# A change of order on two engines: FFN maximum against bias bands on VectorE, left-over keys against AV on TensorE

## The chip, the cores and the metric

The kernel runs on one core of one Trainium2 chip. The metric is device time in microseconds (us) of one execution. Five engines of the core matter here: TensorE (PE in the profile; PEld are its weight loads), VectorE (DVE), ScalarE (ACT), GpSimd (POOL, which here issues the casting loads) and SyncE (SP, which issues stores and DMA transposes). Lines such as L350 are lines of the kernel's source.

## The reference, cut to what matters

Attention with a relative-position bias per head over 8 batches x 8 heads x 576 tokens x 64, then a maxout FFN with three products over the 4608 tokens.

```python
scores = q @ k.T / sqrt(D) + bias[bucket(|i - j|)]        # per batch and head
attn = exp(scores - max) / sum(exp(scores - max))
x = (attn @ v).transpose(...).reshape(B * S, H * D)
h = maximum(maximum(x @ w1, x @ w2), x @ w3)              # [4608, 768]
out = h @ w_out                                           # [4608, 512]
```

## The kernel before

Heads go in pairs: a *step* (b, hp) is batch b and head pair hp, both counted from 0. A step has two halves. Each half is a *visit* (scores of four key tiles against 256 queries on TensorE, exponentials on ScalarE), bias *bands* (VectorE multiplies tile t of the exponentials by exp(bias); only tiles near the diagonal need it), one half of the AV product of the step before, and one *portion* of the FFN of the batch before. 576 is 4 x 128 + 64: the last 64 keys and queries of a head are handled apart, as *left-overs*.

```python
ps_f = ctx.enter_context(tc.tile_pool(name="ps_f", bufs=2, space=PSUM))    # FFN banks
...
def first(fb):       # f: product with w1; ScalarE copies it to m0
    ...
def second(fb):      # m: product with w2; VectorE: m = max(ps1, m0)
    ...
def third(fb):       # g: product with w3; VectorE: hT = max(ps2, m)
    ...
# portions of 512 tokens: [rest, f0, m0], [g0, f1, m1], ... [g4, f5, m5], [g5, None, o0], [o1, o2]

def fill(target, *hooks):      # FFN groups of the next portions, hooks in between
    ...
    for j, group in enumerate(groups):
        while hooks and (j == len(groups) - 1 or j > 0 and len(hooks) > len(groups) - 1 - j):
            hooks.pop(0)()
        group()
    for hook in hooks:
        hook()

def transposes(b):             # SyncE: DMA transposes of a batch's q and k, one t per call
    ...
    for t in range(KT + 1):    # t == KT: the left-over tiles
        one(0, t)              # qT
        one(1, t)              # kT
        yield

def left_keys(hp, qT, kT, el, lo, hi, sc=None):
    ...
        mm(sc[:, q0 - lo : q1 - lo], lhsT=kT[:, KT * P :], rhs=qT[:, q0:q1])
    exp(el[:, lo:hi], sc[:, 0 : hi - lo])
...
    # one step
    together = b > 1 and (b, hp) != (2, 0)
    rate = 8 if b == 1 or (b, hp) == (2, 0) else 13
    visit(qT, kT, e4, 0)                                   # first half
    ...
    quotients = next_late()                                # AV, half 0, of the step before
    times_band(hp, e4, 0, 0, QS, inorder)
    quotients()
    ...
    fill(rate, *([lambda: next_late()()] if together else []),
         lambda: left_keys(hp, qT, kT, el, 0, S))
    times_bandt(hp, el)
    visit(qT, kT, e4, 1, el=el if together else None)      # second half
    ...
    quotients = None if together else next_late()
    times_band(hp, e4, 1, 0, QM, inorder)                  # band 1
    ...
    fill(rate, lambda: times_band(hp, e4, 2, 0, QM, inorder), queries)   # bands 2 and 3
    times_band_left(hp, el)
```

`inorder` keeps an instruction in program order on its engine; matmuls are all in program order.

The softmax here doesn't subtract the row's maximum and nothing guards it: scores larger than these inputs give would overflow.

## Time and profile before

| | before |
|---|---|
| three runs when the work began | 335.92 us median (334.09 to 338.63) |
| span of the profiled run | 332.1 us, granted TensorE clock 1.000 |
| busy: PE, DVE, ACT, POOL | 93%, 64%, 60%, 33% |
| length of a step from batch 3 on, by head pair 0, 1, 2, 3 | 9.08, 8.65, 8.76, 9.08 us |

A line of the view of waits reads: who waited <- for whom: total us, times, longest. A line of the timeline reads: start, duration, engine, line, operation, out<-in, count, and in brackets the engine's idle time before it with what ended it. In part 2 of the page each digit is the busy share of one fortieth of the span, in tenths; the rows of TensorE and the DMA engines show where the two limits lie:

```profile
PE   7987999999999999999999999999999999999995
...
DMA  9999999999999999999949992994031103301103
```

TensorE is nearly full everywhere. The DMA engines are full up to about 200 us but for one slice, full once more from about 208 to 224 us, and mostly idle afterwards. The prediction quotes the waits and one step.

### The profile page before, as it was taken

The numbers are of one execution on the slowest core, as the hardware profiler recorded it, in microseconds if no ns is written. First come the engines' busy times: TensorE is split into PE (matmuls) and PEld (weight loads), VectorE is DVE, ScalarE is ACT, GpSimd is POOL, SyncE is SP. The second block draws the span as 40 slices with busy tenths as digits, with TensorE's granted clock in tenths as the row PEclk, the third lists the DMA queues.
The fourth block names the chain that finished last, engine by engine and source line by source line (L and its number), as shares of the span: only waits on it lengthen the run. The fifth ranks groups of instructions, "written<-read, shape, count | busy, mean of one in ns | idle before, by whom it ended". The sixth has DMA issues, their size and how long they took to land.

```text
span 332.1 us, 8194 instructions
## 1 busy us (share of the span) xinstructions
PE 308.1 (93%) x3288; PEld 171.6 (52%) x3328; DVE 213.6 (64%) x535; ACT 199.5 (60%) x297; POOL 108.0 (33%) x143
## 2 busy tenths in 40 slices
PE   7987999999999999999999999999999999999995
PEld 2455777665544545454555554555445455444442
DVE  6397688776766766676666766776667666545452
ACT  3898888866667666666666666757766561021221
POOL 8931970568466540762048301400000000000000
PEclk9999999999999999999999999999999999999999
DMA  9999999999999999999949992994031103301103
GB/s 169 193 212 197 138 130 168 123 131 198 167 148 158 151 189 162 92 117 201 161 49 130 194 176 35 127 184 96 2 73 66 64 2 63 136 0 57 71 0 126
DMA packets 163878, 40.34 MB, mean 121 GB/s; under 512 B 153720, under 2 KB 159360, under 8 KB 163840
## 3 DMA queue, kind: packets, MB, share of 16 engines
q0 software_dynamic: 103776, 16.66, 75.1%
q1 hardware_dynamic: 58304, 22.69, 37.6%
q10 hardware_dynamic: 1760, 0.47, 0.7%
q8 instruction: 26, 0.43, 0.5%
q14 instruction: 12, 0.10, 0.1%
HBM read 35.39 MB, written 9.45 MB: 135 GB/s over the span
## 4 chain that ended last, share of the span: by engine, by line
PE 63%; ACT 14%; DVE 7%; DMA 7%; issue 4%; POOL 3%; POOLq 0%; ACTq 0%
PE ps L94 30%; PE pso L94 13%; PE a L94 13%; ACT e L530 8%; PE sc L94 6%; DMA xT<-in_q_dram 5%; DVE hT L350 4%; DVE m L345 3%; ACT el L530 3%; ACT m L339 3%; DMA vx<-in_v_dram 1%; PE sct L94 1%; POOL q_sb L139 1%; PE scq L94 1%; PE tp L97 1%
## 5 line engine op out<-in xcount | busy, mean ns | idle before, releaser
L94 PE MATMUL ps<-xT,w_bf 128*128 128x512 bf16 (+1 forms) x694 | 153.7, 357 | 12.4 <-DVE hT L350 9.9
L530 ACT ACTIVATE e<-sc 128x1024 bf16<-128x1024 f32 x128 | 124.5, 1031 | 30.8 <-PE sc L94 30.7
L94 PEld LDWEIGHTS <-w_bf 128*128 128x128 bf16 x720 | 64.1, 97 | 73.5 <-issue 19.8
L524 DVE TENSOR_TENSOR e<-e,hank 128x512 bf16<-128x512 bf16 (+2 forms) x136 | 59.8, 468 | 34.9 <-ACT e L530 34.7
L339 ACT ACTIVATE m<-ps 128x512 bf16<-128x512 f32 x54 | 32.9, 609 | 64.3 <-PE ps L94 61.9
L345 DVE TENSOR_TENSOR m<-ps,m 128x512 bf16<-128x512 f32 x54 | 37.3, 690 | 44.6 <-PE ps L94 23.4
L94 PEld LDWEIGHTS <-kT 64*128 64x128 bf16 (+1 forms) x832 | 30.0, 95 | 36.1 <-issue 25.8
L94 PE MATMUL pso<-wo_bf,hT 128*128 128x512 bf16 (+2 forms) x208 | 47.7, 373 | 0.8 <-issue 0.2
L139 POOL DMA_DIRECT2D vx<-in_v_dram x32 | 28.2, 899 | 62.2 <-PE a L94 60.2
L94 PE MATMUL a<-vx,e 128*128 128x65 bf16 x1024 | 44.5, 193 | 0.0
L94 PE MATMUL sc<-qT,kT 64*128 64x256 bf16 x512 | 41.8, 278 | 2.2 <-ACT e L530 0.9
L94 PEld LDWEIGHTS <-e 128*128 128x128 bf16 x1024 | 40.5, 97 | 3.0
L350 DVE TENSOR_TENSOR hT<-ps,m 128x512 bf16<-128x512 f32 x54 | 37.1, 687 | 4.6 <-PE ps L94 3.1
L94 PE MATMUL a<-vt,el 128*128 128x130 bf16 x160 | 35.6, 222 | 0.0
L632 DVE TENSOR_TENSOR x_sb<-a,rd 128x256 bf16<-128x256 f32 (+1 forms) x64 | 31.4, 491 | 2.2
L94 PEld LDWEIGHTS <-hT 128*128 128x128 bf16 x222 | 20.2, 98 | 23.1 <-issue 1.5
L110 DVE COPY osb<-pso 128x512 f32<-128x512 f32 (+1 forms) x33 | 22.6, 686 | 13.4 <-PE pso L94 9.7
L94 PEld LDWEIGHTS <-el 128*128 128x128 bf16 x416 | 24.0, 97 | 8.8 <-issue 5.9
L530 ACT ACTIVATE el<-scq 128x256 bf16<-128x256 f32 (+1 forms) x55 | 20.5, 416 | 9.9 <-PE scq L94 9.7
L530 ACT ACTIVATE el<-sct 128x576 bf16<-128x576 f32 (+2 forms) x36 | 21.4, 598 | 6.9 <-PE sct L94 6.8
L167 POOL DMA_DIRECT2D q_sb<-in_q_dram x24 | 21.9, 911 | 10.2 <-DMA vx<-in_v_dram 4.7
L167 POOL DMA_DIRECT2D k_sb<-in_k_dram x24 | 21.8, 910 | 6.2 <-DMA vx<-in_v_dram 5.7
(68 smaller groups left out, 160.5 us busy)
## 6 DMA issues: line engine op xcount, KB each, us to landing
out_dram<-osb SPq DMA_DIRECT2D x35, 256.0 KB, 3.0
vx<-in_v_dram POOLq DMA_DIRECT2D x32, 128.0 KB, 6.2
q_sb<-in_q_dram POOLq DMA_DIRECT2D x26, 128.0 KB, 8.8
k_sb<-in_k_dram POOLq DMA_DIRECT2D x24, 128.0 KB, 9.3
w_bf<-in_moe_w_dram POOLq DMA_DIRECT2D x3, 768.0 KB, 13.2
xT<-in_k_dram SPq DMA_DIRECT2D x6, 128.0 KB, 4.6
hank<-w_dr SPq DMA_DIRECT2D x2, 384.0 KB, 6.0
wo_bf<-in_moe_w_out_dram POOLq DMA_DIRECT2D x1, 768.0 KB, 11.9
```

The lines of the kernel that those rows point to most:

```text
L94: inorder(nc.tensor.matmul(*args, **kw))
L97: inorder(nc.tensor.transpose(*args))
L110: return inorder(nc.vector.tensor_copy(out_, in_))
L139: in_turn(b, nc.gpsimd.dma_start(out=dst[:, t, h0:h1, :], in_=x[:, t, h0:h1, :])) for t in range(t0, t1)
L167: loads.append(in_turn(b, nc.gpsimd.dma_start(out=dst[:, t], in_=main_part(src, b)[:, t])))
L339: nc.scalar.activation(out=st[fb]["m0"][:], in_=ps0, func=ACTF.Copy)
L345: inorder(nc.vector.tensor_tensor(out=m[:], in0=ps1, in1=st[fb]["m0"][:], op=ALU.max))
L350: inorder(nc.vector.tensor_tensor(out=hT[:, fb * CH : fb * CH + CH], in0=ps2, in1=st[fb]["m"][:], op=ALU.max))
L524: put(nc.vector.tensor_tensor(out=e4[:, t, :, lo:hi], in0=e4[:, t, :, lo:hi], in1=hank[:, 2 * hp : 2 * hp + 2, c0:c1][:, :, ::-1], op=ALU. ...
L530: nc.scalar.activation(out=out_, in_=in_, func=ACTF.Exp, scale=inv_sqrt_d)
L632: divided[b, hp, half] = inorder(nc.vector.tensor_tensor(out=x_sb[b][:, 2 * half : 2 * half + n, P * hp : P * hp + P].rearrange("p t (h d) ...
```

## The change

The intent: VectorE takes the maximum of the first FFN group (hT) before it turns to the bands that stand behind the second visit; and on TensorE the left-over keys and the second half of AV both stand right behind the first FFN group of the first half. It holds for the steps called `together`, (2,1) to (7,3).

```diff
-        fill(
-            rate, *([lambda: next_late()()] if together else []),
-            lambda: left_keys(hp, qT, kT, el, 0, S),
-        )
+        def keys():
+            left_keys(hp, qT, kT, el, 0, S)
+            if together:
+                next_late()()
+
+        fill(rate, keys, *([lambda: None] if together else []))
...
-        quotients = None if together else next_late()
-        times_band(hp, e4, 1, 0, QM, inorder)
-        if quotients:
+        if not together:
+            quotients = next_late()
+            times_band(hp, e4, 1, 0, QM, inorder)
             quotients()
...
-        fill(rate, lambda: times_band(hp, e4, 2, 0, QM, inorder), queries)
+        def bands_2():
+            for t in range(1 if together else 2, 3):
+                times_band(hp, e4, t, 0, QM, inorder)
+
+        fill(rate, bands_2, queries)
```

First half, before: g, AV, f, keys, m. Now: g, keys, AV, f, m. Second half on VectorE, before: band 1, hT, bands 2 and 3, m. Now: hT, bands 1 to 3, m.

## The prediction

> **What bounds the kernel now.** I read the page's busy shares first, then TensorE's waits, then the timeline of one step. Part 1 of the page:
>
> ```profile
> span 332.1 us, 8194 instructions
> PE 308.1 (93%) x3288; PEld 171.6 (52%) x3328; DVE 213.6 (64%) x535; ACT 199.5 (60%) x297; POOL 108.0 (33%) x143
> ```
>
> TensorE (PE) is busy 93% of 332.1 us, nothing else over 64%. So only two things can move the time: TensorE's idle time, or a delay of its in-order stream. The view of waits between 85 and 275 us, where batches 2 to 7 overlap with the FFN of the batch before (columns: total us, times, longest):
>
> ```profile
> PE ps L94 <- DVE hT L350: 9.9, 17, 0.6
> PE ps L94 <- issue: 1.6, 10, 0.2
> ```
>
> One wait repeats 17 times with nearly the same length and is 9.9 of the 11.5 us that TensorE is seen waiting there: an FFN product waits until VectorE (DVE) has taken the maximum hT. No TensorE wait on a DMA is listed in this stretch. One of the 17, in the timelines of TensorE, VectorE and ScalarE (start, duration, then in brackets the idle time before it):
>
> ```profile
> 82.98 0.60 PE L94 MATMUL sc<-qT,kT 64*128 64x256 bf16 x8
> 83.51 1.90 PE L94 MATMUL ps<-xT,w_bf 128*128 128x512 bf16 x8
> 86.00 1.02 PE L94 MATMUL ps<-xT,w_bf 128*128 128x512 bf16 x4 [0.58 <-DVE hT L350]
> 86.95 0.61 PE L94 MATMUL sc<-qT,kT 64*128 64x256 bf16 x8
> 87.50 0.23 PE L94 MATMUL a<-vt,el 128*128 128x130 bf16 x1
> ```
> ```profile
> 84.79 0.56 DVE L524 TENSOR_TENSOR e<-e,hank 128x768 bf16<-128x768 bf16 x1 [0.90 <-ACT e L530]
> 85.26 0.68 DVE L350 TENSOR_TENSOR hT<-ps,m 128x512 bf16<-128x512 f32 x1
> 85.86 0.88 DVE L524 TENSOR_TENSOR e<-e,hank 128x768 bf16<-128x768 bf16 x2
> 87.13 0.69 DVE L345 TENSOR_TENSOR m<-ps,m 128x512 bf16<-128x512 f32 x1 [0.38 <-PE ps L94]
> ```
>
> Eight FFN matmuls start at 83.51: the first group g (four, the third product of a block, which ends in hT) and f (four, evacuated by ScalarE). The next group m uses g's PSUM bank; the pool has two. VectorE is idle from 83.89, but stands in program order before band 1, which waits for ScalarE's exponential of this visit's scores until 84.79. Only behind that band comes hT, 85.26 to 85.94, and m starts 0.06 later. The band isn't needed by m at all.
>
> **What the Trainium skill says.** (1) "TensorE: Matmul & The Clock Gate", § Architectural detail: VectorE's and ScalarE's queues are strict FIFO. The trace agrees: hT, whose input was done by about 84.58 (below), waited behind a band that started at 84.79. (2) "Perfetto Trace Analysis", § Optimization Strategy: consistent bubbles, the same gap again and again on the engine that should be saturated, can mean that SBUF or PSUM is short for the next tile. The trace agrees: 17 gaps of 0.58 us, each on a PSUM bank. (3) "VectorE: DVE Perf Modes", § Why PSUM operands drop a tier: an fp32 PSUM operand goes at the base rate. hT takes 0.69 us here, against 0.43 for a 512-column band in SBUF; the move makes neither shorter. (4) "Perfetto Trace Analysis", § Per-instruction lifecycle: the window shown for a DMA issued by SyncE leaves out its data movement. The trace agrees: a transpose's issue took 1.22 us, its landing 8.5 (shown below).
>
> **The change part by part.** No instruction is added or removed. It acts on the 23 steps (batch, head pair) whose FFN portions are taken at rate 13: (2,1) to (7,3). Two halves a step, one portion a half.
>
> *Second half: band 1 goes behind the first group.* Where that group is g, hT stands alone. To find when it could start I take the case where it waits for TensorE only: a group g at 212.37, its hT at 213.44, so 1.07 us after g's start. Here 83.51 + 1.07 = 84.58; plus 0.68 for hT and 0.06 to the matmul: m at 85.32 instead of 86.00. f would end its issue at 83.51 + 8 x 0.213 = 85.21, so about 0.1 stays hidden in the pipeline. **Gain 0.68 us a time.** How often: a batch's FFN has eight portions, and counting through the loop (batch 2 starts one portion late) the second halves of head pairs 2, 3 and 0 have [g, f, m], that of pair 1 has two output groups. Pairs 2 and 3 occur for six batches, pair 0 for five: 17, as many as the waits. Sum 17 x 0.68 = **11.6 us**.
>
> What stands after it: bands 1 to 3 then run from g + 1.67; the third ends at g + 3.06 (the second waits for the second exponential at g + 2.18). The next AV wants them at m + 1.49 (86.00 to 87.50), which is now g + 3.30. It still fits, by 0.2 us. ScalarE: two exponentials, the copy m0, left-overs, 6.5 us in a step of 9.07; it idles 1.2 us before the next visit, so it doesn't take over.
>
> *Second half of pair 1.* The copy of the first output group now comes before all three bands. It can start at about 218.54 against the band's 218.31, so the bands end some 0.2 later, at 220.5, where AV wants the last at about 220.46. Loss about 0.1 x 5 = **0.5 us**. At the very end of attention (7,3) AV follows m without a visit between: **0.4 us**.
>
> *First half: left-over keys ahead of the second AV.* The same matmuls in another order: 0.24 us of keys, 0.90 of AV, 0.86 of f. There is no TensorE wait in these halves now, so nothing to gain. The bank for the keys is that of the visit's first scores, whose exponential ends some 1.5 us after the visit's start, the keys come at 2.0: free. But the keys of a batch's first step read the left-over tiles of kT and qT, written by DMA transposes during the batch before, and now need them 0.90 + 0.86 = 1.76 us sooner. For batch 3:
>
> ```profile
> 90.63 1.22 SPq L455 DMA_TRANSPOSE kT<-ktail  x1
> ```
> ```profile
> kT<-ktail SPq DMA_TRANSPOSE x1, 8.5
> ```
> ```profile
> 99.81 0.41 PE L94 MATMUL sct<-qT,kT 128*128 128x512 bf16 x2
> ```
>
> The first is SyncE's timeline, the second the DMA issues of that stretch (median us to landing), the third TensorE's timeline. The last tile lands at 90.63 + 8.5 = 99.1 to 99.2; the keys start at 99.81: 0.6 us of slack. SyncE issues back to back from 66 to 92 us and the DMA engines are full (9 in all 40 slices of 88 to 92), before almost any gain has been made, so the landing doesn't move. Step (3,0) would start 2 x 0.68 sooner, at 94.7 instead of 96.04; the last main tile of kT (landing 95.47 in the trace) costs 0.5; then AV 0.60 and g 0.86 bring the keys to 97.3. They wait until 99.2, nearly 2 us, then 0.24 + 0.90 + 0.86 follow and m starts at 101.2. It was 100.05, and would have been 98.7. **Loss 2.5 us, once.** For batch 4 the tile lands at 131.5 with the keys wanted near 133; for 5 and 6 the SyncE queue is released by stores that move forward with TensorE. I count nothing there.
>
> Sum: 11.6 - 2.5 - 0.5 - 0.4 = 8.2 us.
>
> **Rivals.** (A) *The full gain, 10 to 11.6 us (about 325)*: the transposes move forward too, and keys never wait. For it: no TensorE wait on a DMA now. Against: the slack of 0.6 us against the 1.76 + 1.36 by which keys come sooner. (B) *DMA becomes the bound up to batch 6.* The DMA row reads 9 in all but one of the first 23 slices, up to 191 us. If the loads and transposes run at their own pace, batches 4 to 6 wait as well, and only the gains after about 205 us survive: those of (6,0), (6,2), (6,3) and the three of batch 7, 6 x 0.68 = 4 us, so 332. For it: 75% of the engines' time is the casting loads' queue. Against: the load queue itself waited for AV to free buffers, 60.2 us in four waits, so it has slack and moves forward with TensorE. (C) *VectorE becomes the bound*: bands finish late and AV waits in each of the 17. It is 64% busy, and my margin is 0.2 us; if the sum is off by 0.2, AV loses 0.1 to 0.2 each, 2 to 3 us together: 330. (D) *ScalarE*: the exponentials of a visit can't start sooner than its matmuls, but the visits all move forward together. No loss expected.
>
> **The range and the chances.** 335.9 - 8.2 = 327.7. C and B each cost some, A gains; I shade by half a microsecond: **328.2**. Low end 325.0 is A; high end 331.5 is B or C. The 2% line is 329.2, a gain of 6.7 us. About seven in ten for more, nearly all the rest within 2%, since nothing here lengthens the stream beyond what it gains: faster 0.70, same 0.29, slower 0.01.
>
> **What would show it.** Right: the wait of ps for hT falls from 17 x 0.58 to nearly none; hT starts ahead of band 1, 1.07 us after g; m follows 1.81 after g; a second half with g is 0.68 shorter. One new wait of about 2 us before the left-over keys near 97 us, put down to the transposes of kT or to nothing known; no such wait for batches 4 to 6. TensorE's busy time unchanged. Wrong if new waits on kT, qT or DMA appear in several batches (B), if AV waits for bands (C), or if the keys of batch 3 don't wait (A).

## The result

The changed kernel took 326.0 us (median of four runs, 325.17 to 327.9), the kernel before 337.1 us in the same rounds. A ratio here is the mean time of one kernel's runs over that of the other's of the same rounds, so not quite the ratio of these medians: 0.9689, 95% interval 0.9602 to 0.9777. Executions over 1.5% slower than the fastest of the same kernel are left out of the means. A second timing, in a later job (below), gave 0.9769, 0.9742 to 0.9797, a gain of 7.7 us; there the kernel before spread less. Both say: faster by over 2%.

The profile after, page and waits of TensorE from 85 to 275 us, against the lines that the prediction shows:

```profile
span 324.7 us, 8194 instructions
PE 305.5 (94%) x3288; PEld 171.1 (53%) x3328; DVE 214.1 (66%) x535; ACT 201.1 (62%) x297; POOL 108.1 (33%) x143
```
```profile
PE sc L94 <- DMA kT<-k_sb: 1.9, 1, 1.9
PE sct L94 <- DMA kT<-ktail: 1.3, 2, 1.1
```

The 17 waits for hT are gone. In their place there are three waits for DMA transposes that did not exist before. The step that the prediction showed, in the timelines of TensorE and VectorE:

```profile
83.75 2.84 PE L94 MATMUL ps<-xT,w_bf 128*128 128x512 bf16 x12
86.53 0.61 PE L94 MATMUL sc<-qT,kT 64*128 64x256 bf16 x8
```
```profile
84.83 0.69 DVE L350 TENSOR_TENSOR hT<-ps,m 128x512 bf16<-128x512 f32 x1 [0.70 <-PE ps L94]
85.44 1.40 DVE L524 TENSOR_TENSOR e<-e,hank 128x768 bf16<-128x768 bf16 x3
86.75 0.68 DVE L345 TENSOR_TENSOR m<-ps,m 128x512 bf16<-128x512 f32 x1
```

All twelve FFN matmuls now run as one row without a gap. hT starts 84.83 - 83.75 = 1.08 us after g; the three bands follow it.

Step by step (from one group of left-over queries to the next, so a row holds the second half of the step before and the first half of its own; worked out from the start times in the two traces):

| step | before, us | after, us | difference |
|---|---|---|---|
| (2,3), (3,3), (4,3), (5,0), (5,3), (6,0), (6,3), (7,0), (7,3) | 9.08 each | 8.41 to 8.42 each | -0.66 each |
| (3,1), (4,1), (5,1), (6,1), (7,1) | 8.65 each | 7.98 to 7.99 each | -0.66 each |
| (3,2) to (7,2), five steps | 8.76 each | 8.76 each | 0 |
| from (7,3)'s left-over queries to the end of the last copy | 58.96 | 58.29 | -0.67 |
| (3,0) | 9.08 | 10.85 | +1.77 |
| (4,0) | 9.08 | 9.67 | +0.59 |

Seventeen second halves hold a group g: 17 x 0.66 = 11.2 us won. (3,0) and (4,0) hold one each, so they lost 1.77 + 0.66 = 2.4 us and 0.59 + 0.66 = 1.25 us. 11.2 - 2.4 - 1.25 = 7.55 us; from (2,1) on the two profiled runs differ by 7.6 us (the terms are rounded), and at the start the changed one is 0.24 us behind.

### The profile page after: what moved, and what is told of

It reads as the page before. It is cut to its first block, busy times and chain, and to the rows that moved or that the text cites. A ratio compares the mean times of both kernels' runs of the same rounds, so it can differ in the third digit from the quotient of the medians.

```text
span 324.7 us, 8194 instructions
## 1 busy us (share of the span) xinstructions
PE 305.5 (94%) x3288; PEld 171.1 (53%) x3328; DVE 214.1 (66%) x535; ACT 201.1 (62%) x297; POOL 108.1 (33%) x143
## 4 chain that ended last, share of the span: by engine, by line
PE 74%; DMA 8%; SPq 5%; ACT 4%; POOL 3%; DVE 3%; issue 2%; ACTq 0%; POOLq 0%
PE ps L94 38%; PE a L94 12%; PE pso L94 12%; PE sc L94 7%; DMA kT<-ktail 5%; SPq L455 4%; ACT e L530 3%; PE sct L94 2%; DMA vt<-in_v_dram 2%; PE scq L94 2%; DVE e L524 1%; POOL q_sb L139 1%; POOL vx L139 1%; DMA out_dram<-osb 1%; PE tp L97 1%
## 5 line engine op out<-in xcount | busy, mean ns | idle before, releaser
L94 PE MATMUL ps<-xT,w_bf 128*128 128x512 bf16 (+1 forms) x694 | 151.2, 357 | 1.4
L94 PEld LDWEIGHTS <-w_bf 128*128 128x128 bf16 x720 | 65.2, 97 | 64.1 <-issue 8.4
L524 DVE TENSOR_TENSOR e<-e,hank 128x512 bf16<-128x512 bf16 (+2 forms) x136 | 59.0, 470 | 14.3 <-ACT e L530 12.9
L94 PE MATMUL a<-vx,e 128*128 128x65 bf16 x1024 | 46.0, 195 | 0.0
L94 PE MATMUL sc<-qT,kT 64*128 64x256 bf16 x512 | 40.8, 272 | 4.9 <-DMA kT<-k_sb 1.9
L94 PEld LDWEIGHTS <-e 128*128 128x128 bf16 x1024 | 41.7, 99 | 0.9
```

The source lines that it names most:

```text
L94: inorder(nc.tensor.matmul(*args, **kw))
L524: put(nc.vector.tensor_tensor(out=e4[:, t, :, lo:hi], in0=e4[:, t, :, lo:hi], in1=hank[:, 2 * hp : 2 * hp + 2, c0:c1][:, :, ::-1], op=ALU. ...
```

## The experiments

The kernel before ran beside each kernel in the same rounds; its mean was 334.4, 335.1, 334.8 and 334.8 us in the four jobs (numbers 1 to 4, 5 to 8, 9 to 11, 12). Each job ran on another chip, so kernels of different jobs are compared by their ratios. All twelve results were correct. The theory: **program order on VectorE made the 17 waits, and on its new, earlier schedule TensorE meets DMA transposes that are not early enough.** The main rivals: the moved keys are a part of the gain; the DMA waits come from the competing loads; the DMA is simply the bound. By the prediction's account the wait needs both the band ahead of hT and a pool of only two banks; a third bank was not tried.

| kernel | ratio to before | 95% interval | mean, us below before |
|---|---|---|---|
| changed, again | 0.9769 | 0.9742 to 0.9797 | 7.7 |
| bands only | 0.9701 | 0.9664 to 0.9738 | 10.0 |
| changed, keys late in first steps | 0.9727 | 0.9689 to 0.9764 | 9.2 |
| keys only | 1.0056 | 1.0013 to 1.0099 | -1.7 |
| two bands first | 1.0122 | 1.0067 to 1.0177 | -3.7 |
| bands only, batch-4 loads later in program | 0.9714 | 0.9663 to 0.9765 | 9.7 |
| changed, batch-4 loads later in program | 0.9749 | 0.9717 to 0.978 | 8.5 |
| before, batch-4 loads later in program | 0.9982 | 0.9945 to 1.002 | 0.7 |
| bands only, batch-4 loads gated | 0.9719 | 0.9695 to 0.9743 | 9.7 |
| bands only, transposes in order of need | 0.9659 | 0.9635 to 0.9683 | 11.7 |
| the same, first visit late | 0.9701 | 0.9671 to 0.973 | 10.4 |
| changed, transposes in order of need | 0.9764 | 0.972 to 0.9807 | 7.6 |

### 1. The changed kernel again (control)

No edit.

> The changed kernel as it is, as the control on this chip. My theory (17 waits of TensorE for the hT maximum at 0.66 us removed, 11.2 us; 2.4 us given back in step (3,0) and 1.2 us in step (4,0) to waits for DMA transposes): 7 to 8 us below the kernel before. Rival, from the medians of the first timing: 10 to 11 us below, something in the kernel before is slower on most runs than in its profiled one.

Measured: 326.65 us mean, 7.7 us below. The size that the theory gave from the traces (7 to 8 us) holds; the 10 to 11 us of the first timing came from a kernel before that ran at 337.1 us there and at 334.3 here. Its own profiled run shows something new. It hardly waited in (3,0), because it had come 5.8 us late into (2,1):

```profile
73.11 0.27 PE L94 MATMUL a<-vt,el 128*128 128x130 bf16 x1 [3.04 <-DMA vt<-in_v_dram]
74.18 2.75 PE L94 MATMUL pso<-wo_bf,hT 128*128 128x512 bf16 x6
```
```profile
75.00:77.00 2.00, 2.00 (x6) 0.76 (x5) 0.08 (x2) 0.00 (x0) 2.00 (x4) 0.50 2.31 170
```

The first fence is TensorE's timeline, the second a stretch of 2 us (busy time of each engine, then granted clock, DMA share, GB/s). AV waited 3.04 us for a load of v, and then six matmuls took 2.75 us instead of 1.46: the granted clock was 0.50, from 72.1 to 78.9 us by the trace's clock records. The wait is of a load that lands between about 68 and 73.1 us in different runs, when AV wants it near 70. No changed step has run by then, so I take it for run-to-run noise. But it shows that **a wait of TensorE can cost more than its own length.**

### 2. The second half alone: bands only

```diff
 (the changed kernel, with the first half's old fill put back)
-        fill(rate, keys, *([lambda: None] if together else []))
+        fill(rate, *([lambda: next_late()()] if together else []),
+             lambda: left_keys(hp, qT, kT, el, 0, S))
```

> Only the second half of the change: hT ahead of band 1; keys and AV of the first half in the old order. My theory: all 17 waits for hT go, and the two waits for the left-over tile of kT in (3,0) and (4,0) go too (0.2 + 1.1 us), while the wait of 1.9 us for the last main tile of kT in (3,0) stays: 1 to 1.5 us below the changed kernel. Rival (moving the keys frees ScalarE or a PSUM bank and is needed): slower than the changed kernel, with waits for ScalarE or VectorE in the first halves.

Measured: 10.0 us below the kernel before, 2.3 us below the changed kernel; two of its six runs were slow (329.0 and 329.3 us) and are left out, and the intervals only just part. With all six runs its mean is 326.0 us, 8.4 below the kernel before and only 0.7 below the changed kernel: how far it beats the changed kernel is not settled by these times. All 17 waits for hT are gone and so are those for the left-over tile. This is the clean test of the main step: against the kernel before nothing changed in TensorE's order, only in VectorE's, and each of the steps with g went from 9.08 to 8.41. The wait for the main tile stayed, as expected, and the clock halved after it:

```profile
97.63 0.28 PE L94 MATMUL sc<-qT,kT 64*128 64x256 bf16 x2 [1.75 <-DMA kT<-k_sb]
```
```profile
99.00:101.00 2.00, 2.00 (x14) 1.03 (x13) 0.90 (x3) 0.00 (x0) 2.00 (x3) 0.50 2.34 153
```

Step (3,0) took 11.96 us, 3.55 more than the undisturbed 8.41: 1.75 of wait, and 3.4 us at half clock (98.1 to 101.5), which cost half of that, 1.7. In the changed kernel's profiled run a wait of 1.87 us at the same place was not followed by a lower clock. So the same stall costs 2 or 3.5 us from run to run. That is likely what splits this kernel's runs into 322.9 to 324.0 and 326.7 to 329.3; only the run of 326.74 has a trace, so the others are argued, not shown. If it is so, the two runs left out are a cost of this kernel too.

### 3. Keys late in the first step of each batch

```diff
+        if hp:
             fill(rate, keys, *([lambda: None] if together else []))
+        else:
+            fill(rate, *([lambda: next_late()()] if together else []),
+                 lambda: left_keys(hp, qT, kT, el, 0, S))
```

> The changed kernel, but in the first step of each batch the left-over keys stand where they stood before. My theory: the waits for the left-over kT tile vanish in (3,0) and (4,0), the same time as the bands-only kernel, 1 to 1.5 us below the changed kernel. Rival: if the transposes are simply the bound, the wait comes back elsewhere and the time is that of the changed kernel.

Measured: 9.2 us below, between the changed kernel and bands only; step (3,0) took 9.10 us with waits of 0.2 and 0.2, step (4,0) 8.41. The new order in the other steps neither gains nor loses against bands only within the intervals. In the profiled run the wait did not come back elsewhere. But there the last main tile landed at 96.2 us, against 97.3 in the changed kernel, and the step began 0.7 us later, so a part of the shorter waits is luck; and the interval overlaps that of the changed kernel. This run alone doesn't exclude the rival; number 12 tests the place of the keys better.

### 4. The first half alone: keys only

```diff
 (the kernel before, with the first half of the change)
+        fill(rate, keys, *([lambda: None] if together else []))
```

> Only the first half of the change: keys and AV behind the first FFN group, bands as before. My theory: the 17 waits of 0.58 us for hT stay; in (3,0) the keys come at 98.1 instead of 99.8 and wait about 1.2 us for the tile that lands at 99.2 to 99.3: 1 to 1.3 us above the kernel before (0.3 to 0.4%). Rival (this half brings a part of the gain): below the kernel before.

Measured: 1.7 us above the kernel before (ratio 1.0056). TensorE's waits:

```profile
PE ps L94 <- DVE hT L350: 9.9, 17, 0.6
...
PE sc L94 <- DMA kT<-k_sb: 1.1, 1, 1.1
```

The 17 waits stay at 9.9 us: this half brings none of the gain. In (3,0) it lost 1.8 us, 1.1 of it for a main tile of kT, which in this run was late by itself, and 0.3 for the left-over tile; I had expected the whole loss at the left-over tile. The place of the wait was wrong, the sign and nearly the size right.

### 5. One more band in the way: two bands first

```diff
 (the kernel before)
         times_band(hp, e4, 1, 0, QM, inorder)
+        if together:
+            times_band(hp, e4, 2, 0, QM, inorder)
...
-        fill(rate, lambda: times_band(hp, e4, 2, 0, QM, inorder), queries)
+        def band_2():
+            if not together:
+                times_band(hp, e4, 2, 0, QM, inorder)
+
+        fill(rate, band_2, queries)
```

> The kernel before with bands 1 and 2 ahead of the first FFN group in the second halves (one more band in VectorE's way). My theory (strict program order on VectorE makes the wait): hT starts 2.65 us after the first group instead of 1.75, so each of the 17 waits grows from 0.58 to about 1.48 us: 15 us above the kernel before (up to 17 with the copies of pair 1). Rival (the wait is set by the PSUM bank or TensorE and the band only fills idle time): within 2 us of the kernel before.

A miss: 3.7 us above the kernel before, not 15. The waits, and one step on TensorE, VectorE and ScalarE:

```profile
PE ps L94 <- ACT m L339: 13.5, 17, 0.8
```
```profile
141.39 1.02 PE L94 MATMUL ps<-xT,w_bf 128*128 128x512 bf16 x4 [0.80 <-ACT m L339]
```
```profile
141.35 0.68 DVE L350 TENSOR_TENSOR hT<-ps,m 128x512 bf16<-128x512 f32 x1
```
```profile
140.71 0.63 ACT L339 ACTIVATE m<-ps 128x512 bf16<-128x512 f32 x1
```

hT did move as worked out, by 0.9 us. But group m starts at 141.39, while hT is still running (to 142.03), and 0.05 us after ScalarE's copy of f had ended (140.71 + 0.63 = 141.34). So m no longer used g's bank; with two banks in the pool it must have been given f's when the program was built. The wait grew only from 0.58 to 0.80, and 17 x 0.22 = 3.7 us is what was measured. The dose that I meant to give was not given; the run shows instead that **a change of order can change which bank a later tile gets.**

### 6 to 8. The loads of batch 4, later in the program

```diff
-        if hp == 2 and 1 < b < B - 2:
+        if hp == (3 if b == 2 else 2) and 1 < b < B - 2:
             batch[b + 2] = load_tiles()
             load_qk(b + 2)
```

On bands only:

> The bands-only kernel with the loads of q and k for batch 4 issued one step later, (2,3) instead of (2,2), away from the DMA transposes of batch 3. My theory (those loads share the DMA engines with the transposes and make them late): the last main tile of kT lands before 95.5 us, the wait of 1.8 us in (3,0) and the half clock after it go, step (3,0) takes 8.4 us instead of 9.1 to 12; 11 us below the kernel before, ratio 0.965 to 0.968. Rival (SyncE's own issue rate sets the landing): still a wait of 1 to 2 us in (3,0), the time of bands-only; or the late loads bring a new wait in (4,0).

On the changed kernel:

> The changed kernel with the same later loads. My theory: the main tiles are in time, and the left-over tile must land before 96.9 us not to be waited for; it follows two transposes behind, so a wait of 0 to 1 us stays in (3,0) and perhaps in (4,0): 10 to 11 us below the kernel before. Rival: as bands_qk4, no effect, 7.7 us below.

On the kernel before:

> The kernel before with the same later loads, as control. My theory: nothing waited for these transposes there, so the time is that of the kernel before within 0.5%. Rival (the loads cost time in themselves): faster by 1 us or more.

No effect on any of the three within the intervals (0.9714 against 0.9701; 0.9749 against 0.9769; 0.9982 against 1). On bands only the wait was there as before, and longer:

```profile
PE sc L94 <- DMA kT<-k_sb: 2.4, 1, 2.4
```

The reason was mine: GpSimd issued the first of those loads at 87.5 us against 88.5 in bands only (first line bands only, second line this run):

```profile
88.52 0.90 POOL L167 DMA_DIRECT2D q_sb<-in_q_dram  x1 [0.21 <-DMA ktail<-in_k_dram]
```
```profile
87.53 0.90 POOL L167 DMA_DIRECT2D q_sb<-in_q_dram  x1 [0.19 <-issue]
```

It has nothing of the step to wait for, so a later place in the program is not a later time. The three runs say nothing on contention, and the third is hardly a control: its loads began at 87.4 us against 86.25 in the kernel before, 1.2 us later where a step was meant.

### 9. The same loads, held back by a dependency

```diff
 (bands only, with the edit of numbers 6 to 8)
-            load_qk(b + 2)
+            load_qk(b + 2, turned_qk[3, 1, KT] if b == 2 else None)
```

> The bands-only kernel where the loads of q and k for batch 4 wait for the last transpose of batch 3. The later program position of bands_qk4 did nothing to their time: GpSimd, which waits for no step, issued them at 87.5 us as before. This gate moves them truly, to about 96 us. Contention theory: the last main tile of kT lands 1 us or more sooner than 97.6 to 98.1, the wait of 1.8 to 2.4 us in (3,0) shrinks below 1 us, unless the loads then come late for the transposes of batch 4 (a wait in (4,0)). Rival (the transposes queue behind each other and behind the v loads only): the wait in (3,0) stays at 1.5 us or more, time as bands-only, ratio 0.970.

Measured: 9.7 us below, as bands only. The gate worked (GpSimd's timeline), and the wait stayed (TensorE's waits from 66 to 140 us):

```profile
99.39 0.90 POOL L167 DMA_DIRECT2D q_sb<-in_q_dram  x1 [13.55 <-DMA kT<-ktail]
```
```profile
PE sc L94 <- DMA kT<-k_sb: 2.6, 1, 2.6
```

The loads began at 99.4 us, the last main tile of kT landed at 98.3, no sooner than the 97.6 to 98.1 of the runs with loads beside it. The loads of batch 4 are not the cause. What else lands in these 10 us are the v loads of batch 3 (98.4 for the last) and the transposes themselves, one behind the other; which of the two sets the pace is left open.

### 10. The transposes in the order of need

```diff
-        for t in range(KT + 1):
-            one(0, t)
-            one(1, t)
+        for pair in (((0, 0), (1, 0)), ((0, 1), (1, 1)), ((1, 2), (1, 3)), ((0, 2), (0, 3)), ((0, KT), (1, KT))):
+            for j, t in pair:
+                one(j, t)
             yield
```

The first visit of a batch needs all key tiles, but only the first two query tiles.

> The bands-only kernel with the DMA transposes of a batch in the order in which they are needed: the last two key tiles ahead of the last two query tiles, left-over tiles last as before. Theory (they land one after another, about 1.2 to 1.8 us apart, whatever is in them): the last main key tile lands two places sooner, at about 95, so the first visit of (3,0) waits 0 to 0.5 us instead of 1.8 to 2.4; the keys later in the step then wait 0 to 1 us for the left-over tile at 99.8 to 100.2. 1 to 2 us below bands-only, more where TensorE's clock no longer halves: ratio 0.965. Rival (the landing of everything slips together): no change.

Measured: 11.7 us below the kernel before, ratio 0.9659, and the five runs lie between 322.66 and 323.53 us. The last main key tile landed at 91.8 us instead of 97.6. The profiled run had no wait for it, the full clock from 14 to 320 us, and one wait for the left-over tile, which landed at 98.75 (put down to ScalarE, which had long been done):

```profile
98.79 0.42 PE L94 MATMUL sct<-qT,kT 128*128 128x512 bf16 x2 [0.63 <-ACT m L339]
```

(3,0) took 9.21 us, 0.8 more than undisturbed. This is the lowest ratio of all; it beats the kernel before and the changed one, but its interval overlaps that of bands only.

### 11. First visit behind AV and the first FFN group as well

```diff
+        behind = together and hp == 0
+        if not behind:
             visit(qT, kT, e4, 0)
...
+        def first_visit():
+            visit(qT, kT, e4, 0)
+            times_band(hp, e4, 0, 0, QS, inorder)
+
+        def keys():
+            next_late()()
+            left_keys(hp, qT, kT, el, 0, S)
+
+        if behind:
+            fill(rate, first_visit, keys)
+        else:
+            ...
```

> As bands_kfirst, and in the first step of each batch the visit stands behind the first AV and the first FFN group, which need nothing of the new batch: 1.46 us of other work before the new tiles are needed. Theory: no wait above 0.3 us for the main tiles in (3,0), the left-over tile still 0 to 1 us, no half clock there: 0 to 1 us below bands_kfirst, ratio 0.963 to 0.966. Rival (the later visit makes ScalarE's exponentials late): new waits for ScalarE in the five first steps, slower than bands_kfirst.

Measured: 10.4 us below, 1.3 us worse than the version without it; the intervals overlap a little. The profiled run shows no wait for ScalarE that would bear out the rival. In (3,0) it waited 0.39 us before the left-over keys, and the step took 8.97 us, 0.24 less than in number 10. But it lost 0.8 us in (2,0), which the edit does not touch: there the keys waited 1.0 us for the left-over tile of batch 2. Why the six runs are no better is not settled. Once the key tiles are in time, the extra room buys nothing that shows.

### 12. The changed kernel with the transposes in the order of need

The edit of experiment 10 on the changed kernel.

> The changed kernel (keys early) with the transposes in the order of need. My theory: the wait for the main key tile in (3,0) goes, but the early keys want the left-over tile at about 96.5 us and it lands at 98.7 to 99.8: one wait of 2 to 3 us in (3,0) and 0.5 to 1 us in (4,0) take its place, so the time stays near that of the changed kernel, ratio 0.973 to 0.977, well above bands_kfirst at 0.966. Rival (the order of the transposes alone brought the gain of bands_kfirst, the place of the keys is indifferent): ratio 0.966.

Measured: 7.6 us below, ratio 0.9764, as the changed kernel and not as number 10. TensorE's timeline in (3,0), and two stretches of 4 us (the third number from the end is the granted clock):

```profile
96.09 1.02 PE L94 MATMUL ps<-xT,w_bf 128*128 128x512 bf16 x4
100.29 0.66 PE L94 MATMUL sct<-qT,kT 128*128 128x512 bf16 x2 [3.17 <-DMA kT<-ktail]
```
```profile
98.00:102.00 4.00, 1.71 (x22) 1.44 (x23) 0.00 (x0) 0.65 (x1) 4.00 (x6) 0.77 2.16 154
102.00:106.00 4.00, 3.78 (x36) 1.97 (x35) 1.61 (x4) 1.48 (x4) 2.25 (x3) 0.80 1.94 159
```

The main tiles came in time, and the early keys waited 3.17 us for the left-over tile, which landed at 100.24. The clock then stood at half from 100.1 to 103.6, and the step took 13.29 us: 4.88 more than 8.41, 3.17 + 1.7. The order of the transposes pays only where the keys come late. With number 10 this shows the cost of the moved keys directly: 323.1 against 327.2 us, the same kernel otherwise. (In the two profiled runs the left-over tile also landed at different times, 98.75 and 100.24 us, so 1.5 us of the longer wait is not the place of the keys.)

## Why the prediction was right

*The removed wait* was right in mechanism and nearly in size: 17 times, hT 1.08 us after g (1.07 predicted), 0.66 us each (0.68), shown by the trace after and by bands only.

*The new wait in (3,0)* was right in total and wrong in its parts. Predicted: 2.5 us, of it 0.5 for the last main tile and 2.0 for the left-over tile. The profiled run lost 2.4 us, but 1.87 for the main tile and 0.22 for the left-over one. The step that failed is to take the landings from the trace before. For the left-over tile, of which I wrote "so the landing doesn't move", it held in this run (99.3 us against 99.1); but the last main tile, which I put at 95.47, landed at 97.3. Its landing moves, from run to run and kernel to kernel, between 95.5 and 98.4 us. The waits share one stream: what is lost at the first is not lost again at the second.

*Batch 4*, for which I counted nothing, lost 1.25 us: its left-over tile landed at 134.2 instead of 131.5, when the keys wanted it at 133.1. So the sign "no such wait for batches 4 to 6" failed for batch 4; batches 5 and 6 were free: DMA didn't become the bound.

*The two small losses* that I subtracted, 0.5 for pair 1 and 0.4 at the end, did not occur: (3,2) to (7,2) stayed at 8.76, and the end gained its full 0.67. In pair 1 of batch 6 the bands did end later, as worked out: 0.23 us after AV's first matmul had started (216.45 against 216.22), where before they ended 0.01 ahead of it. Yet AV shows no gap; which of its matmuls reads the last band the trace doesn't show. These 0.9 us and the 1.25 of batch 4 nearly cancel, so that the sum of 8.2 is so near to the 7.6 of the traces and the 7.7 of the control is in part luck. The absolute 328.2 us was 1.6 to 2.2 too high. It starts from 335.9, the median of three runs; the kernel before ran at 337.1 in the first timing and at 334.3 in the control, so the start is uncertain by more than that.

*A small slip*: the prediction spaces f's matmuls by 0.213 us; in the trace before they start 0.218 apart (83.51 to 85.04 over seven), so f's issue would end at about 85.26 and not 85.21. The gain doesn't rest on it.

*What the prediction lacked*: that a stall of 1.75 to 3.2 us can come with half the clock for 3.4 us or more. It needed no such term for the profiled run, but it is a part of the spread.

*The rivals*: DMA as the bound (B) shows in two steps only; VectorE as the bound (C) nowhere; the full gain (A) only when the keys stay late and the transposes come in the order of need, 11.7 us. Busy time of TensorE was said to stay the same; it fell from 308.1 to 305.5 us, which I take for the modelled ends of matmuls before gaps, without a test.

## What to carry to other kernels

When an engine takes its work in strict order, put what frees a buffer for the busiest engine ahead of work that merely has to be done, above all if that work may itself wait. Before moving a consumer forward, look up when each of its inputs lands, not only whether somebody waits today: the left-over tile, with 0.6 us of slack before, became a stall of 3.17 us in number 12. Issue transfers in the order in which they are needed, and hold one back with a dependency, not with a later line in the program.

## What the Trainium skill lacked or had wrong

- "TensorE: Matmul & The Clock Gate", § The HAM clock gate and § HAM oscillation, says that the clock drops after an idle window of about 3.4 us, and that gaps above some 3.4 us are to be avoided. Here gaps of 1.75 us (bands only), 2.4 us (number 6), 3.04 us (the changed kernel again) and 3.17 us (number 12) came with 3.4, 3.4, 6.8 and 3.4 us at a granted clock of 0.5, which began within 0.5 us after the gap or inside it, while gaps of 1.87 us (the changed kernel) and 2.6 us (number 9) came with the full clock. The two levels of clock, 1.0 and 0.5, and the unit of 3.4 us agree with the page; the length of gap that is safe does not.
- "DMA: Bandwidth & Descriptors", § DMA Transpose (X-bar), gives no time from issue to landing under load. For the left-over tile of kT it was 8.5 us in batch 3 with the DMA engines full and 2.4 us in batch 7 with them idle (kernel before), with an issue of 1.2 us in both.
